# Attention with pooled upsampling and a mixer of eight batches: the scale of u from a bound in place of its largest value, and a new order table

## The chip, the cores and the metric

One core of a Trainium2 chip runs the program. The metric is the device time of one execution in microseconds; lower is better. The kernel before takes 911.1 us, the median of three runs (910.91 to 912.58).

## What is computed

For each of 8 batches the reference adds two attentions of 8 heads over 576 positions (head size 64), and runs a mixer with two pairs of matrices over the result:

```
q_d, k_d, v_d = means over groups of 4 positions (576 -> 144)
out_up    = repeat(softmax(q_d k_d^T / 8) v_d, 4)
out_local = softmax(mask(|i - j| < 4, q k^T / 8)) v
x = (out_up + out_local), laid out as 576 x 512
u = x + (relu(x^T w_tok1) w_tok2)^T          # w_tok1 576 x 256, w_tok2 256 x 576
y = u + relu(u w_ch1) w_ch2                  # w_ch1 512 x 1536, w_ch2 1536 x 512
```

All inputs and outputs are f32 in value; the weights arrive as 64-bit words and are converted on the chip.

## The kernel before

Every large product is made of three 16-bit passes (`mm3`, line 132): each operand is split into a high f16 part and a low f16 part (the rest), after it was multiplied with a power of two that keeps it in f16's range. So each operand needs a scale, and a scale needs a number that no value exceeds.

**Start.** Batch 0's attention runs while the weights load. Each weight tile is converted by `to_f32` (line 232): an activation on ScalarE, two passes on GpSimd (lines 242 and 245), one on VectorE (line 250). `token_weight` and `column_sums` make the token weights W: TensorE sums magnitudes (`W_sum`, line 304), VectorE turns the largest into a scale (`wscale`), and both split the tiles (lines 279 and 281). `load_v` squares V on ScalarE (line 503) and pools it on GpSimd (lines 507 and 508); `value_scale` (line 318) makes from it the factors `up` and `down` of a batch, and the products `av` with V (line 657) wait for them through `st.up`. `C1` and `C2` (w_ch1 and w_ch2, 12 tiles each) are converted, scaled (`root`, line 147) and split (`parts`, line 368).

**Mixer.** `mix(st)` (line 682) is the token mixing of a batch: `splits` splits x, `products` forms t1 = w_tok1 with x (line 710), `takes` writes `hid` = relu of it as two f16 parts (lines 739 and 741), `products` forms t2 on top of the transposed x (lines 723 and 728), and `takes` reads it out of PSUM as u (line 752). Batch 0 then goes on in `scaled`, the others in `mixtures`, `upper` and `lower`, which also form sums of blocks of u: batches 1 to 7 do the first channel product with seven products in place of eight (`product7`, tensors P, Q and R). `second` forms the second channel product (tensor c with weights CX), `second_up` adds u (line 1042) and stores.

**The scale of u** is the part that the change touches. Per column block c and chunk of positions ch VectorE reads all of u again for its largest magnitude:

```
nc.vector.tensor_reduce(st.umx[:, ch, c:c + 1], st.u[c][:, s0:s0 + N], axis=AX.X, op=ALU.max, apply_absolute_value=True)
```

That is 8 instructions a batch, 64 in all (line 754). `scale_of` (line 758) then makes one number of them in `everywhere` (line 666): a maximum on VectorE, a transposition on TensorE (`um_t`), a maximum of the row, a product with ones that spreads it (`um_b`), and `pow2` (line 136), three small VectorE instructions. Batch 0 does this once per chunk, the others once.

**What sets the order.** The kernel writes its instructions as some 300 streams (attention pieces b, mixer pieces n, channel pieces e, the start's A, C, D, W and others). `drive` (line 180) merges them before the program is built: it keeps a clock per engine from estimated step lengths, and of the streams that could go next at about the same time takes the one that stands first in ORDER. Each engine then executes its instructions strictly in that written order, so ORDER decides what stands behind what in each queue. Until batch 0's first scale is made, `keep_busy` puts products with `junk` (tensor `busy`, line 178) where the estimate sees TensorE idle.

Of the kernel before, what the change touches and what calls it, by code (L numbers as in the profile page):

```python
# [6 lines left out]
F32 = mybir.dt.float32  # L7
# [26 lines left out]
SWITCH = 0.1  # L34
SHARED = 1.4
ORDER = ("C1 e3.1 e5.5 e5.3 A7 e3.5 e3.3 s1 e5.0 e5.6 e5.4 D11 L1 n6.3 n7.0 b3.9 e2.4 e7.1 e3.0 e3.6 e3.4 "
# [9 lines left out]
         "b3.3 e2.2 C11 b6.5 Q0 D9 h2 C7 b5.3 N2 C2 e4.7 e3.7 e6.7 C3 e1.7 n6.5 e5.7 ").split()  # L46
# [7 lines left out]
def tile_ups_attention_mixer(ctx, tc, qk, vw, vr, w1, w2, c1, c2, out):  # L54
# [15 lines left out]
    BUFS = dict(cw=6, h=6, vm=2, bs=2, bs2=4, w=4, xh=2, x=5, u=6, uh=7, tm=6, ts=2, qk=4, qd=1, vw=2, vd=1, pt=2, od=1, sm=10, ev=4, nm=4, qs=1, sc=20)  # L70
# [89 lines left out]
    def step(engine, us, *needs, at=None, take="", give=""):  # L160
        return dict(F="P", W="V").get(engine, engine), us, needs, at, take.split(), give.split(), engine
# [156 lines left out]
    def value_scale(st):  # L318
# [6 lines left out]
        e = yield step("V", 0.8, give="g")  # L325
        root(big, 2.0 ** 20, st.big[:, 0:1], st.big[:, 1:2])
        nc.vector.tensor_mul(st.up, whole[:, 0:1], st.big[:, 1:2])
        nc.vector.tensor_mul(st.down, whole[:, 1:2], st.big[:, 0:1])
        make(("scale", b), e)
# [48 lines left out]
    class First(Channel):  # L378
# [8 lines left out]
        def scale(self):  # L387
            for q in range(NQ):
# [4 lines left out]
                root(big, 2.0 ** (4.5 + 0.5 - 8), self.inv[q], self.s[q])  # L393
# [272 lines left out]
    def everywhere(name, cols, n=128):  # L666
# [512 lines left out]
```

## Time and profile before

| what | value |
|---|---|
| median of three runs | 911.1 us |
| the profiled execution's own time | 909.63 us |
| its span, first to last instruction | 907.8 us |
| TensorE busy | 869.8 us, 96% of the span |
| VectorE busy | 551.3 us, 61% |
| ScalarE busy | 438.3 us, 48% |
| GpSimd busy | 303.2 us, 33% |
| mean granted TensorE clock | 0.985 |

A share over the whole span mixes stages with different limits, so the tables of stretches and the timelines tell more than this one. A busy TensorE is not a TensorE at its peak, and its fillers with `junk` count as busy too.

### The profile page before, as it was taken

How to read it: one execution, taken by the hardware profiler on the slowest of the kernel's cores; microseconds unless marked ns; L12 is line 12 of the kernel's file. 1: busy time of each engine (PE TensorE's matmuls, PEld its weight loads, DVE VectorE, ACT ScalarE, POOL GpSimd, SP SyncE). 2: the span in 40 equal slices, each digit the busy share in tenths (PEclk: the TensorE clock that was granted, in tenths of full speed). 3: DMA queues.
4: the chain of work that ended last, by engine and by line, in shares of the span. 5: the costliest groups of instructions: out<-in, count | busy, mean ns of one | idle time of the engine just before them, and what ended most of it. 6: DMA issues, size and time to landing. Idle time of an engine off the chain costs nothing.

```text
span 907.8 us, 26395 instructions
## 1 busy us (share of the span) xinstructions
PE 869.8 (96%) x11183; PEld 656.0 (72%) x11189; DVE 551.3 (61%) x1306; ACT 438.3 (48%) x1028; POOL 303.2 (33%) x465
## 2 busy tenths in 40 slices
PE   6877799999999999999999999999999999999998
PEld 3644568867676877777877777778877786787776
DVE  6778999678863764447653485445854584524521
ACT  4656467344663545534563455535463555503510
POOL 4779874399004420054015220054004420002000
PEclk9769999999999999999999999999999999999999
DMA  9844541363125111450156002441126211110201
GB/s 256 217 168 165 187 114 35 116 187 103 56 97 177 48 37 57 140 148 22 52 174 141 23 21 74 142 132 43 50 67 198 69 35 43 53 44 24 74 20 34
DMA packets 36870, 87.23 MB, mean 96 GB/s; under 512 B 4464, under 2 KB 17264, under 8 KB 35504
## 3 DMA queue, kind: packets, MB, share of 16 engines
q1 hardware_dynamic: 36112, 84.95, 30.7%
q8 instruction: 88, 1.44, 0.7%
q10 hardware_dynamic: 640, 0.59, 0.2%
q14 instruction: 30, 0.25, 0.1%
HBM read 71.37 MB, written 11.80 MB: 92 GB/s over the span
## 4 chain that ended last, share of the span: by engine, by line
PE 81%; DVE 11%; ACT 4%; issue 2%; DMA 1%; POOL 0%; SPq 0%; ACTq 0%; DVEq 0%; POOLq 0%
PE c L134 31%; PE P L134 13%; PE t L134 10%; PE R L134 7%; PE Q L134 3%; PE av L657 3%; PE ad L587 3%; PE t L723 2%; PE pT L644 2%; PE sc L621 2%; PE sd L559 2%; PE td L578 1%; DMA vr<-in_vr_dram 1%; DVE CX L250 1%; ACT pd L571 1%
## 5 line engine op out<-in xcount | busy, mean ns | idle before, releaser
L134 PE MATMUL c<-h,CX 128*128 128x320 f16 (+1 forms) x2304 | 296.8, 286 | 0.0
L134 PEld LDWEIGHTS <-CX 128*128 128x128 f16 x2304 | 221.4, 98 | 59.1 <-issue 4.0
L134 PEld LDWEIGHTS <-CW 128*128 128x128 f16 x1296 | 123.4, 98 | 38.9 <-issue 2.9
L533 POOL TENSOR_TENSOR qs<-qk 128x288 f32<-128x288 f32 x56 | 40.3, 719 | 246.2 <-DMA qk<-in_qk_dram 242.4
L1042 DVE SCALAR_TENSOR_TENSOR u<-c,io,u 128x256 f32<-128x256 f32 (+1 forms) x64 | 32.9, 514 | 93.0 <-PE c L134 92.3
L134 PEld LDWEIGHTS <-t 128*128 128x128 f16 x756 | 73.9, 98 | 19.3 <-issue 0.6
L507 POOL TENSOR_TENSOR vr<-vr 72x256 f32<-72x256 f32 x64 | 48.2, 754 | 77.5 <-ACT dump L503 77.0
L752 ACT ACTIVATE u<-t,down 128x256 f32<-128x256 f32 (+1 forms) x64 | 29.9, 497 | 84.2 <-PE t L134 84.2
L134 PE MATMUL t<-xh,W 128*128 128x512 f16 (+1 forms) x240 | 58.0, 379 | 0.0
L754 DVE TENSOR_REDUCE umx<-u 128x1 f32<-128x256 f32 (+1 forms) x64 | 28.0, 448 | 45.6 <-ACT u L752 45.5
L947 DVE TENSOR_TENSOR x<-x,Q 128x288 f32<-128x288 f32 x42 | 19.0, 452 | 59.7 <-PE Q L134 59.6
L134 PE MATMUL t<-W,hid 128*128 128x256 f16 (+1 forms) x384 | 53.5, 286 | 0.3 <-DVE hid L741 0.3
L571 ACT ACTIVATE pd<-sd,nmd 72x144 f32<-72x144 f32 x128 | 37.7, 373 | 33.0 <-DVE nmd L566 28.7
L503 ACT ACTIVATE dump<-vr 72x512 uint8<-72x512 f32 x64 | 40.1, 627 | 26.9 <-DMA vr<-in_vr_dram 26.4
L801 POOL TENSOR_TENSOR s<-u,u 128x288 f32<-128x288 f32 x14 | 11.1, 810 | 123.1 <-ACT u L752 123.1
L701 DVE SCALAR_TENSOR_TENSOR xh<-x,back,xh 128x512 f16<-128x512 f32 (+1 forms) x40 | 32.7, 824 | 22.5 <-ACT xh L699 22.4
L134 PEld LDWEIGHTS <-hid 128*128 128x128 f16 x384 | 36.2, 98 | 9.6 <-DVE hid L741 0.6
L587 PE MATMUL ad<-vd,ptd 72*72 72x65 f32 x512 | 40.7, 234 | 0.3 <-ACT ptd L581 0.3
L587 PEld LDWEIGHTS ad<-vd,ptd 72*72 72x72 f32 x512 | 39.0, 151 | 2.2 <-ACT ptd L581 0.8
L662 ACT ACTIVATE x<-av,up 128x512 f32<-128x512 f32 (+1 forms) x40 | 27.3, 685 | 25.1 <-PE av L657 24.7
L134 PE MATMUL P<-a22h,CW 128*128 128x288 f16 x252 | 38.0, 286 | 1.4 <-DVE m L947 1.2
L134 PEld LDWEIGHTS <-W 128*128 128x128 f16 (+1 forms) x240 | 21.9, 97 | 24.0 <-issue 3.1
(182 smaller groups left out, 1658.1 us busy)
## 6 DMA issues: line engine op xcount, KB each, us to landing
qk<-in_qk_dram SPq DMA_DIRECT2D x32, 579.0 KB
t<-sums SPq DMA_DIRECT2D x42, 384.0 KB
vw<-in_vw_dram SPq DMA_DIRECT2D x32, 351.0 KB
vr<-in_vr_dram SPq DMA_DIRECT2D x64, 144.0 KB
C_raw<-in_c_dram SPq DMA_DIRECT2D x16, 512.0 KB
out_dram<-u SPq DMA_DIRECT2D x32, 160.0 KB
C_raws<-in_c_dram SPq DMA_DIRECT2D x8, 512.0 KB
out_dram<-u SPq DMA_DIRECT2D x32, 128.0 KB
```

Source lines behind the costliest of these rows:

```text
L134: nc.tensor.matmul(ps, lhs(a), rhs(c), start=first and i == 0, stop=last and i == 2, **kw)
L503: nc.scalar.activation(dump, t.rearrange("p r c -> p (r c)"), AF.Square, scale=2.0 ** -20, accum_out=st.vm[:, i:i + 1])
L507: nc.gpsimd.tensor_add(t[:, 0:2], t[:, 0:2], t[:, 2:4])
L533: nc.gpsimd.tensor_add(two, x[:, :, 0:2], x[:, :, 2:4])
L571: nc.scalar.activation(pd[:, par, g], s[:, par, g], AF.Exp, bias=nm[:, par, g:g + 1], scale=0.125 / 16)
L587: nc.tensor.matmul(ps[:, g, par], pt[:, par, kg, G * g:G * g + G], st.vd[:, kg, 2 * pr + par], start=kg == 0, stop=kg == 1)
L657: nc.tensor.matmul(ps[QB * j:QB * j + QB, par, D * hp:D * hp + D], pt[p, hp, QB * j:QB * j + QB], st.vw[h][p, g, D * hp:D * hp + D], start ...
L662: nc.scalar.activation(x.rearrange("p hp two d -> p two hp d"), ps[:n, :, :4 * D].rearrange("p two (hp d) -> p two hp d", hp=4), AF.Copy, ...
L701: nc.vector.scalar_tensor_tensor(st.xh[t][:, 1], xf(t), back[:n], st.xh[t][:, 0], ALU.mult, ALU.subtract)
L752: nc.scalar.activation(st.u[c][:, s0:s0 + N], banks[ch, c // 2][:, c % 2, :N], AF.Copy, scale=st.down)
L754: nc.vector.tensor_reduce(st.umx[:, ch, c:c + 1], st.u[c][:, s0:s0 + N], axis=AX.X, op=ALU.max, apply_absolute_value=True)
L1042: nc.vector.scalar_tensor_tensor(u, banks[c, ch], io[:, ch:ch + 1], u, ALU.mult, ALU.add)
```

## The change

u is not read again for its largest value. u is `down` times (x and the token mixing), so a bound on it comes from numbers that are there earlier: the largest v (`big`), and the largest value of `hid` times the largest column sum of w_tok2, which `whole` already carries. `value_scale` writes two factors into a new tile `most`, and `scale_of` takes one maximum over both halves of `hid`'s high parts, spreads it as before, and forms bound = largest hid x most[1] + most[0]. One scale serves both chunks of batch 0 now. The powers of two beside it move (2^-5 to 2^-7 for u, 2^-8 to 2^-6 for C1) and so do two buffer counts. The table ORDER and the constant SWITCH, the planner's price for a change of kind on TensorE, are other ones, so nearly every engine's order changes.

```
-SWITCH = 0.1
+SWITCH = 0.05
-ORDER = ("C1 e3.1 e5.5 e5.3 A7 e3.5 e3.3 s1 e5.0 e5.6 e5.4 D11 L1 n6.3 n7.0 b3.9 e2.4 e7.1 e3.0 e3.6 e3.4 "
...
+ORDER = ("n3.2 e1.1 e3.1 e6.1 D7 b3.2 e5.1 e7.1 A2 e6.2 D4 e6.5 b6.8 b5.3 e4.1 b4.8 b6.3 n6.2 e1.4 T0 e5.2 "
...
-    BUFS = dict(... bs2=4 ... sc=20)
+    BUFS = dict(... bs2=6 ... sc=16)
...
+        st.most = T([128, 2], F32, "bs2", f"most{b}")
+        nc.vector.tensor_scalar(st.most[:, 0:1], st.big[:, 0:1], 4.0, None, ALU.mult)
+        nc.vector.tensor_scalar(st.most[:, 1:2], st.down, 516.0, None, ALU.mult)
...
-                root(big, 2.0 ** (4.5 + 0.5 - 8), self.inv[q], self.s[q])
+                root(big, 2.0 ** (4.5 + 0.5 - 6), self.inv[q], self.s[q])
...
+            st.tops = both[:, :, 0]
             make(("hid", b), e)
-            st.umx = T([128, 2, 4], F32, "sc", f"umx{b}")
...
-                    e = yield step("V", 0.05 + N * 0.00112)
-                    nc.vector.tensor_reduce(st.umx[:, ch, c:c + 1], st.u[c][:, s0:s0 + N], axis=AX.X, op=ALU.max,
-                                            apply_absolute_value=True)
...
+        def scale_of():
+            yield step("V", 0.0, ("hid", b))
+            big = yield from everywhere(f"um{b}", st.tops, 128, 1.1)
+            inv = st.ui[0] = st.ui[1] = T([128, 1], F32, "sc", f"ui{b}")
+            s = T([128, 1], F32, "sc", f"us{b}")
+            most = T([128, 1], F32, "sc", f"mu{b}")
+            yield step("V", 0.55, give="g")
+            nc.vector.tensor_scalar(most, big, st.most[:, 1:2], st.most[:, 0:1], ALU.mult, ALU.add)
+            pow2(most, 2.0 ** -7, inv, s)
+            return s
```

Three places show what the new order moves. The line numbers of the kernel after are 3 or 4 higher.

The first is GpSimd's queue at the start, from its first work on loaded data; `vr` is V (the pooling sums), `W..._raw` are the token weights (their conversion). Before:

```order
L507 TENSOR_TENSOR vr0_0_195<-vr0_0_195 72x256
L508 TENSOR_TENSOR vd0_191<-vr0_0_195 72x2x64
L242 TENSOR_SCALAR W0_raw_197<-W0_raw_197 128x256
L507 TENSOR_TENSOR vr0_1_199<-vr0_1_199 72x256
L508 TENSOR_TENSOR vd0_191<-vr0_1_199 72x2x64
L507 TENSOR_TENSOR vr0_2_206<-vr0_2_206 72x256
L508 TENSOR_TENSOR vd0_191<-vr0_2_206 72x2x64
L507 TENSOR_TENSOR vr0_3_210<-vr0_3_210 72x256
L508 TENSOR_TENSOR vd0_191<-vr0_3_210 72x2x64
```

After:

```order
L242 TENSOR_SCALAR W0_raw_195<-W0_raw_195 128x256
L245 TENSOR_SCALAR W0_raw_195<-W0_raw_195 128x256
L242 TENSOR_SCALAR W0_raw_195<-W0_raw_195 128x256
L510 TENSOR_TENSOR vr0_0_197<-vr0_0_197 72x256
L511 TENSOR_TENSOR vd0_191<-vr0_0_197 72x2x64
L245 TENSOR_SCALAR W0_raw_195<-W0_raw_195 128x256
L242 TENSOR_SCALAR W2_raw_206<-W2_raw_206 128x256 x2
L242 TENSOR_SCALAR W4_raw_232<-W4_raw_232 64x256
L245 TENSOR_SCALAR W2_raw_206<-W2_raw_206 128x256
L245 TENSOR_SCALAR W4_raw_232<-W4_raw_232 64x256
```

Of V only one tile's sums are left among the conversions, and the last conversion of a weight tile stands behind five tiles of V; before, the sums of four tiles of V (vr0 to vr3) stood ahead of the second weight tile, and the last conversion stood behind all eight.

The second is VectorE's queue in batch 0 around the scale of u; `hid0` and `u0` are batch 0's, `CW` and `CX` are the tiles of C1 and C2, `C1_inv` and `C1_s` the scale of C1's first four tiles. Before, from the first reduction of `u0` on:

```order
L754 TENSOR_REDUCE umx0_1180<-u0_0_1219 128x1
L250 SCALAR_TENSOR_TENSOR CX0_1211<-C2_raw0_1054 128x512
L250 SCALAR_TENSOR_TENSOR CX1_1212<-C2_raw1_1066 128x512
L754 TENSOR_REDUCE umx0_1180<-u0_1_1235 128x1
L374 SCALAR_TENSOR_TENSOR CW3_148<-CW4_149,C1_s0_135,CW3_148 128x512
L754 TENSOR_REDUCE umx0_1180<-u0_2_1259 128x1
L366 TENSOR_REDUCE C1_mx_131<-C1_sum4_1134 128x1
L670 TENSOR_REDUCE C1_n1_m_1275<-C1_mx_131 128x1
L754 TENSOR_REDUCE umx0_1180<-u0_3_1276 128x1
L250 SCALAR_TENSOR_TENSOR CX2_1213<-C2_raw3_1092 128x512
L676 TENSOR_REDUCE C1_n1_m1_1284<-C1_n1_t_1282 1x1
L670 TENSOR_REDUCE um0_0_m_1293<-umx0_1180 128x1
```

After, from the first of VectorE's two writes of `hid0` on:

```order
L744 SCALAR_TENSOR_TENSOR hid0_1158<-t1_0_1033,hid0_1158 128x512
L250 SCALAR_TENSOR_TENSOR CW10_155<-C19_raw_1047 128x512
L744 SCALAR_TENSOR_TENSOR hid0_1158<-t1_0_1033,hid0_1158 128x512
L149 TENSOR_SCALAR C1_inv0_132<-C1_n0_b_1167 128x1
L151 TENSOR_SCALAR C1_inv0_132<-C1_inv0_132 128x1
L152 RECIPROCAL C1_s0_135<-C1_inv0_132 128x1
L673 TENSOR_REDUCE um0_m_1198<-hid0_1158 128x1
L377 SCALAR_TENSOR_TENSOR CW0_145<-CW1_146,C1_s0_135,CW0_145 128x512
L679 TENSOR_REDUCE um0_m1_1212<-um0_t_1210 1x1
L766 TENSOR_SCALAR mu0_1228<-um0_b_1224,most0_840 128x1
L138 TENSOR_SCALAR ui0_1226<-mu0_1228 128x1
L139 TENSOR_SCALAR ui0_1226<-ui0_1226 128x1
```

The maximum over `hid0` stands right behind hid's last write, and its chain has one split of C1 (`CW0`) in it; before, the chain began behind four reductions of u with conversions of C2 between them.

The third is VectorE's queue in batch 2, after its token mixing; `u1` is batch 1's u, to which the second channel product is added. Before (the maximum `um2_0_m` that begins the chain follows 57 rows further down):

```order
L741 SCALAR_TENSOR_TENSOR hid2_4376<-t1_2_4204,hid2_4376 128x512
L1040 TENSOR_TENSOR io1_1764<-ui1_0_3499,ic_158 128x1
L1042 SCALAR_TENSOR_TENSOR u1_0_3241<-c2_1_0_0_4315,io1_1764,u1_0_3241 128x256
L741 SCALAR_TENSOR_TENSOR hid2_4376<-t1_2_4204,hid2_4376 128x512
L565 TENSOR_REDUCE mxd3_0_4410<-sd3_0_4405 72x4
L566 TENSOR_SCALAR nmd3_0_4411<-mxd3_0_4410 72x4
L754 TENSOR_REDUCE umx2_4404<-u2_0_4438 128x1
L754 TENSOR_REDUCE umx2_4404<-u2_1_4458 128x1
```

After:

```order
L744 SCALAR_TENSOR_TENSOR hid2_4338<-t1_2_4222,hid2_4338 128x512 x2
L1043 TENSOR_TENSOR io1_1828<-ui1_3076,ic_158 128x1
L1045 SCALAR_TENSOR_TENSOR u1_0_3028<-c2_1_0_0_4307,io1_1828,u1_0_3028 128x256
L673 TENSOR_REDUCE um2_m_4386<-hid2_4338 128x1
L568 TENSOR_REDUCE mxd3_0_4393<-sd3_0_4388 72x4
L569 TENSOR_SCALAR nmd3_0_4394<-mxd3_0_4393 72x4
L679 TENSOR_REDUCE um2_m1_4404<-um2_t_4402 1x1
L766 TENSOR_SCALAR mu2_4434<-um2_b_4430,most2_3695 128x1
```

The maximum of hid stands behind one addition to batch 1's u, and the whole chain to the scale now follows at once.

## Rows read from the trace of the kernel before

**Rows 1.** The page: busy tenths of TensorE in 40 slices of the span.
```profile
PE   6877799999999999999999999999999999999998
```

**Rows 2.** Stretches: us; PE, PEld, DVE, ACT, POOL busy (count); granted clock; DMA.
```profile
0.00:57.85 57.85, 42.33 (x506) 24.91 (x510) 43.94 (x106) 33.71 (x79) 39.61 (x67) 0.82 0.74 206
57.85:132.58 74.73, 61.71 (x890) 41.55 (x893) 66.72 (x134) 45.10 (x94) 60.61 (x67) 0.95 0.47 167
132.58:228.10 95.52, 94.52 (x1335) 73.04 (x1334) 77.32 (x178) 45.60 (x108) 60.99 (x97) 1.00 0.38 112
228.10:873.00 644.90, 639.82 (x8207) 492.06 (x8205) 359.15 (x883) 313.84 (x749) 141.96 (x235) 1.00 0.26 79
```

**Rows 3.** Timeline, 42 to 62 us: start, us, engine line op; idle before it.
```profile
42.26 1.28 ACTq L603 DMA_DIRECT2D vw<-od  x1
...
45.46 0.76 POOL L245 TENSOR_SCALAR W_raw<-W_raw 128x256 bf16<-128x256 f32 x1
...
50.09 1.39 PE L304 MATMUL W_sum<-W_raw,junk 128*128 128x256 bf16 x5 [2.69 <-ACT W_raw L276]
...
53.65 4.27 DVE L281 SCALAR_TENSOR_TENSOR W<-W_raw,wscale,W 128x256 f16<-128x256 f32 x5
...
57.85 0.14 DVE L670 TENSOR_REDUCE vm_m<-vm 72x1 f32<-72x8 f32 x1
...
62.05 2.05 PE L657 MATMUL av<-vw,pt 47*32 47x64 f32 x128
```

**Rows 4.** VectorE's groups by shape: count, busy us, mean ns, idle before.
```profile
L754 DVE TENSOR_REDUCE umx<-u 128x1 f32<-128x320 f32 x32 | 14.9, 482 | 27.1 <-ACT u L752 27.1
...
L754 DVE TENSOR_REDUCE umx<-u 128x1 f32<-128x256 f32 x32 | 13.1, 415 | 18.5 <-ACT u L752 18.3
...
L250 DVE SCALAR_TENSOR_TENSOR CW<-C_raw 128x512 uint32<-128x512 uint32 x12 | 10.5, 887 | 0.0
...
L281 DVE SCALAR_TENSOR_TENSOR W<-W_raw,wscale,W 128x288 f16<-128x288 f32 x4 | 3.5, 922 | 0.4 <-ACT W L279 0.4
...
L676 DVE TENSOR_REDUCE um_m<-um_t 1x1 f32<-1x128 f32 x9 | 2.5, 273 | 0.4 <-PE um_t L673 0.4
```

**Rows 5.** VectorE's groups by shape, 57.85 to 132.58 us alone.
```profile
L633 DVE TENSOR_TENSOR P<-P,mx 128x304 f32<-128x304 f32 x2 | 1.2, 620 | 0.1
...
L628 DVE TENSOR_TENSOR P<-sc,mask 128x304 f32<-128x304 f32 x2 | 0.9, 458 | 0.0
```

**Rows 6.** Timelines: TensorE around the first product with c1, VectorE at C2's scale.
```profile
96.71 1.89 PE L178 MATMUL busy<-junk 128*128 128x512 bf16 x7 [1.83 <-DVE C_inv L149]
...
99.30 1.47 PE L134 MATMUL c<-uh,CW 128*128 128x256 f16 x12
...
132.58 0.14 DVE L149 TENSOR_SCALAR ic<-C_n_b 128x1 uint32<-128x1 uint32 x1
```

**Rows 7.** Line 250 in the second stretch; lines 250 and 754: ns minimum/median/maximum.
```profile
57.85:132.58 74.73, 20.67 (x22) 0.95 0.47 167
...
L250 DVE SCALAR_TENSOR_TENSOR CW<-C_raw x12: 670/692/1559, 44.2 to 81.6; 128x512 uint32<-128x512 uint32 x12
...
L754 DVE TENSOR_REDUCE umx<-u x64: 402/443/489, 84.1 to 821.5; 128x1 f32<-128x256 f32 x32, 128x1 f32<-128x320 f32 x32
```

**Rows 8.** TensorE's timeline, 112 to 117 us.
```profile
112.82 1.80 PE L134 MATMUL c<-uh,CW 128*128 128x320 f16 x12
114.56 0.71 PE L559 MATMUL sd<-qd 64*72 64x144 f32 x8
115.20 1.80 PE L134 MATMUL c<-uh,CW 128*128 128x320 f16 x12
116.84 0.67 PE L578 MATMUL td<-ident,pd 72*72 72x72 f32 x8
```

**Rows 9.** Batch 0: last product of the token mixing, and VectorE's last write of hid.
```profile
75.52 1.62 PE L134 MATMUL t<-xh,W 64*128 64x512 f16 x6
...
79.50 0.69 DVE L741 SCALAR_TENSOR_TENSOR hid<-t,hid 128x512 f16<-128x512 f32 x1 [0.66 <-ACT hid L739]
```

More of the change, by code (lines that the diff above doesn't have):

```diff
@@ L33 @@
 HOP = 0.2
-SWITCH = 0.1
+SWITCH = 0.05
 SHARED = 1.4
-ORDER = ("C1 e3.1 e5.5 e5.3 A7 e3.5 e3.3 s1 e5.0 e5.6 e5.4 D11 L1 n6.3 n7.0 b3.9 e2.4 e7.1 e3.0 e3.6 e3.4 "
[9 rows of a table removed]
-         "b3.3 e2.2 C11 b6.5 Q0 D9 h2 C7 b5.3 N2 C2 e4.7 e3.7 e6.7 C3 e1.7 n6.5 e5.7 ").split()
+ORDER = ("n3.2 e1.1 e3.1 e6.1 D7 b3.2 e5.1 e7.1 A2 e6.2 D4 e6.5 b6.8 b5.3 e4.1 b4.8 b6.3 n6.2 e1.4 T0 e5.2 "
[9 rows of a table added]
+         "b5.0 C5 e2.7 e5.3 s0 C2 P1 e7.7 Q0 b5.5 e5.7 n2.1 e6.7 e1.7 e4.7 b2.4 ").split()
 PX = 7
@@ L69, in tile_ups_attention_mixer @@
     psum = ctx.enter_context(tc.tile_pool(name="psum", bufs=1, space=bass.MemoryType.PSUM))
-    BUFS = dict(cw=6, h=6, vm=2, bs=2, bs2=4, w=4, xh=2, x=5, u=6, uh=7, tm=6, ts=2, qk=4, qd=1, vw=2, vd=1, pt=2, od=1, sm=10, ev=4, nm=4, qs=1, sc=20)
+    BUFS = dict(cw=6, h=6, vm=2, bs=2, bs2=6, w=4, xh=2, x=5, u=6, uh=7, tm=6, ts=2, qk=4, qd=1, vw=2, vd=1, pt=2, od=1, sm=10, ev=4, nm=4, qs=1, sc=16)
     SLOTS = dict(gg=2, m=3, g=1, w=4)
@@ L324, in value_scale @@
         st.up, st.down = (T([128, 1], F32, "bs2", f"{x}{b}") for x in ("up", "down"))
-        e = yield step("V", 0.8, give="g")
+        e = yield step("V", 1.0, give="g")
         root(big, 2.0 ** 20, st.big[:, 0:1], st.big[:, 1:2])
@@ L664, in local, with everywhere @@
         make(("x", b, t), e)
-    def everywhere(name, cols, n=128):
+    def everywhere(name, cols, n=128, us=0.08, *needs):
         m = T([n, 1], F32, "ev", f"{name}_m")
-        yield step("V", 0.08)
-        nc.vector.tensor_reduce(m, cols, axis=AX.X, op=ALU.max)
+        yield step("V", us, *needs)
+        nc.vector.tensor_reduce(m, cols, axis=AX.X if len(cols.shape) == 2 else AX.XY, op=ALU.max)
         yield step("F", 0.11, take="g")
@@ L748, in takes @@
                 for c in (2 * two, 2 * two + 1):
-                    yield step("A", 0.06 + N * 0.00113, ("t2", b, ch, c), give=f"gg>{b}" if c % 2 else "")
+                    e = yield step("A", 0.06 + N * 0.00113, ("t2", b, ch, c), give=f"gg>{b}" if c % 2 else "")
                     if ch == 0:
@@ L752, in takes @@
                     nc.scalar.activation(st.u[c][:, s0:s0 + N], banks[ch, c // 2][:, c % 2, :N], AF.Copy, scale=st.down)
-                    e = yield step("V", 0.05 + N * 0.00112)
-                    nc.vector.tensor_reduce(st.umx[:, ch, c:c + 1], st.u[c][:, s0:s0 + N], axis=AX.X, op=ALU.max,
-                                            apply_absolute_value=True)
                     make(("u", b, ch, c), e)
-        def scale_of(ch, cols):
-            big = yield from everywhere(f"um{b}_{ch}", cols)
-            inv = st.ui[ch] = T([128, 1], F32, "sc", f"ui{b}_{ch}")
-            s = T([128, 1], F32, "sc", f"us{b}_{ch}")
-            yield step("V", 0.45, give="g")
-            pow2(big, 2.0 ** -5, inv, s)
+        def scale_of():
[7 more added lines that the diff above has]
+            pow2(most, 2.0 ** -7, inv, s)
             return s
@@ L768, in scaled @@
                 s0, N = CHUNKS[ch]
-                yield step("V", 0.0, *(("u", b, ch, c) for c in range(4)))
-                s = yield from scale_of(ch, st.umx[:, ch])
+                if ch == 0:
+                    s = yield from scale_of()
                 uh = st.uh[ch] = []
                 for c in range(4):
-                    yield step("A", 0.06 + N * 0.00113, *([("h", b - 1, ch, NF - 1)] if b else []))
+                    yield step("A", 0.06 + N * 0.00113, ("u", b, ch, c), *([("h", b - 1, ch, NF - 1)] if b else []))
                     if ch == 1 or c % 2 == 0:
@@ L806, in upper @@
         def upper():
+            st.us = yield from scale_of()
             yield step("V", 0.0, *all_u)
-            st.us = yield from scale_of(0, st.umx.rearrange("p a c -> p (a c)"))
-            st.ui[1] = st.ui[0]
             for name in ORDER7:
```

18 rows, old and new, of the table ORDER are left out of this document.

## Prediction

> **What bounds the kernel now.** I read the page's slices first, then a table of four stretches, then the timeline of the start, and the groups of VectorE last. The slices show TensorE at nine tenths or more from about 110 us to the end, and at six to eight tenths ahead of that [rows 1]. The stretches say the same in numbers: from 228.10 to 873 us TensorE is busy 639.82 of 644.90 us at a granted clock of 1.00, while VectorE is busy 359.15; from 132.58 to 228.10 it is busy 94.52 of 95.52. In the two stretches ahead it is not the bound: 42.33 of 57.85 us and 61.71 of 74.73, part of that fillers, and VectorE (43.94 and 66.72) and GpSimd (39.61 and 60.61) carry as much or more [rows 2]. So the kernel is a start of 132.58 us, paced by conversions on VectorE and GpSimd, and then TensorE's own work. Whatever VectorE saves behind 132.58 us is worth nothing unless TensorE waits for it; there only TensorE's work counts.
>
> I cut the start at two instructions that exist in both kernels. The first is the maximum of batch 0's V at 57.85 us: the products with V wait for what follows from it and begin at 62.05 [rows 3]. The second is the start of C2's scale at 132.58 us, the edge of the stretches, from where TensorE is full. The profiled execution took 909.63 us; its median of three is 911.1, so 1.5 is added at the end.
>
> **The change, part by part.** *Removed in the steady part.* 64 reductions of u go, 32 of 0.482 and 32 of 0.415 us, 28.0 us of VectorE in all, and one of nine chains to a scale [rows 4]. *Added:* eight maxima over hid's high parts, 128x1024 in 16 bits each, and three small instructions a batch of some 0.15 us. No reduction over 16-bit values is in this trace. Through the two reductions of u runs a line of 0.067 us more for 64 elements, 1.05 ns an element, which puts 1024 elements at 1.22 us; if 16-bit values were read faster it might be no more than two of the 256-wide reductions, 0.8. I take 1.22, since the nearest rows are of the same instruction. The Trainium skill ("VectorE: DVE Perf Modes", section on the perf-mode tier table) lists this reduction with the slowest mode alone, for every type; by that the 0.8 would drop out, and no row here shows it. Behind 132.58 us about 24 us of 28 fall away, next to a TensorE that waits 5.1 us in 645 [rows 2]: worth 0 there, bounds 0 to -2.
>
> *First piece, to V's maximum.* GpSimd's queue converts the token weights ahead of most of V's sums now, where before V stood ahead. In the timeline GpSimd's last conversion of W begins at 45.46 us, TensorE sums W at 50.09 after 2.69 us of waiting, VectorE then splits five tiles of W from 53.65 on for 4.27 us, and only behind them comes V's maximum [rows 3]. Ahead of that maximum VectorE's queue holds three instructions fewer in the new order: two conversions of C1 at 0.887 and one split of W2 at 0.922 us [rows 4], 2.7 us. Times the stretch over its busy time (57.85 / 43.94 = 1.32) that is -3.6 us. Following the chain by hand along the new queues, with the durations of the rows, V's maximum lands near 51.3 us, 6.5 earlier. Against it: the four transfers `vw`, issued from 42.26 us on and long landed before [rows 3], now stand just ahead of the products with V, whose result needs them. I take -4.5, bounds 0 and -6.5.
>
> *Second piece, to C2's scale.* VectorE's work between the two cuts, each instruction at its group's mean: eight reductions of u out, 4 x 0.482 + 4 x 0.415 = -3.6; one chain of 0.27 and three small ones out, -0.7; one maximum over hid for two small ones, 1.22 - 0.30 = +0.9; three small additions, +0.45; from the first piece two conversions of C1 and one split of W2, +2.7 [rows 4]; one split of C1 less and some writes of h more, -0.3; and two softmax tiles of batch 1, six instructions each, the first group 0.9 and the largest 1.2 us for the two, 5.4 in all [rows 5], which stand behind the cut now, where TensorE is full. The sum is -5.9, on 70.3 us by group means that took 74.73: x 1.06 = -6.3 us. The place where it is felt is the first product with c1. Before, TensorE waited 1.83 us, ran seven fillers at 96.71 us, and began that product at 99.30; C2's scale followed at 132.58 [rows 6]. In the new order those products stand directly behind the token mixing, without fillers. What speaks for less is that VectorE's time here is not all work: line 250 took 20.67 us for 22 conversions where its fastest, 0.670, would make 14.7, and it reaches 1.559 us, while reductions of u stay between 0.402 and 0.489 [rows 7]. The 6 us above the fastest are waits beside GpSimd that do not shrink with VectorE's list. I take -5.0, bounds 0 and -6.3.
>
> The Trainium skill ("SBUF — State Buffer", section "Who interferes with whom") says that a VectorE instruction with two inputs in SBUF and GpSimd's reads exclude each other, while a reduction never contends. The trace agrees, by the spread of line 250 against that of line 754 [rows 7]. It speaks against the change: what is removed are the instructions that were not in GpSimd's way.
>
> *What TensorE has left at C2's scale.* By the two queues, four more groups of c at 128x256 are done by then (1.47 each [rows 6]), two fewer at 128x320 (1.80) and five fewer f32 groups of about 0.67 [rows 8]: 3.6 + 3.4 - 5.9 = +1.1 us later. *Changes of kind.* From batch 1's first product on, TensorE's queue goes from f16 products to f32 ones 141 times, before 125. What one costs is seen only by difference: the same group of c runs 1.74 us until a product `sd` begins (112.82 to 114.56) and 1.64 until `td` does (115.20 to 116.84) [rows 8]. I take 0.10 each, +1.6; bounds 0 and +4, if a change cost the whole overlap of a group with its neighbours, about 0.23. The count of products themselves is the same.
>
> *The chain that moves earlier in TensorE's queue.* The transposition in the scale's chain now stands soon behind the token mixing. In batch 0, hid is whole 3.05 us after the mixing's last product ends (75.52 + 1.62 to 79.50 + 0.69 [rows 9]); with the maximum, 1.22, and some 0.2 between engines, 4.5 us. In five of the seven later batches 36 products of c and one `sd`, about 3 x 1.64 + 0.7 = 5.6 us at most and 5.1 at least [rows 8], stand between. That hides it, with 0.6 to 1.1 us to spare; costed at nothing.
>
> **Sum.** -4.5 - 5.0 + 1.1 + 1.6 = -6.8 us on 909.63, so 902.8; with the 1.5 to the median, **904.3 us**. This case's own range is 899 to 909.
>
> **Rivals.** *One: GpSimd paces the second piece.* If VectorE's waits beside GpSimd grow into the room that is freed, the second piece stays as long as it was. For it: GpSimd is busy 60.61 of 74.73 us there [rows 2] with the same work. Against it: TensorE's wait of 1.83 us and its fillers ended on VectorE. -4.5 + 1.1 + 1.6 = -1.8 gives 909.3. This rival is what the Trainium skill's section cited above ("SBUF — State Buffer", "Who interferes with whom") would make of the piece. Chance 0.14.
>
> *Two, slower: both start pieces keep their length.* In the first GpSimd's 39.61 us and the loads that it waits for (DMA share 0.74 [rows 2]) then set the pace, and the new order only swaps which of V and W is late; the `vw` transfers are late in place of the weights. What remains is the added work of TensorE, +1.1 + 1.6 = +2.7: 913.8. It decides once the two pieces together shorten by less than 2.7 us. Chance 0.14.
>
> *Three: TensorE waits for the scale's chain.* If the maximum over hid runs late, because an addition to the previous batch's u or a softmax stands ahead of it, or it takes 1.9 and not 1.22 us, the cover is used up and TensorE stands about 0.7 us in each of seven batches: +4.9, so 909.2. Against it: VectorE is busy 56% of that stretch [rows 2]. Chance 0.12.
>
> **How the numbers follow.** The forecast has 0.60. A measurement of this kernel can tell about 0.2%, 1.8 us, from no change, so faster begins below 909.3 and slower above 912.9. Faster: 0.57 of the forecast's 0.60 and half of rivals one and three, 0.13, together 0.70. Slower: most of rival two, 0.13. The rest, 0.17, is no change. The range of 898.5 to 912 takes in the forecast's bounds, rivals one and three, and leaves out rival two and the forecast's far tails.
>
> **What would show it.** Right: in the new profile the products with V begin near 58 us (62.05 before), c1's first product follows the token mixing without fillers, C2's scale is made near 123 us (132.58), and from there to the end the time is some 2.7 us longer than before with TensorE waiting about 5 us in the steady part. Wrong: C2's scale at 130 us or later, GpSimd's conversions as the releaser of VectorE's waits, or waits of TensorE ahead of the transpositions `um_t` of several us in sum. A maximum over hid at 0.8 us would leave the sum as it is; one near 2 us would bring rival three.

## The result and the profile after

The kernel after takes 900.97 us, the median of four executions (900.7 to 902.88), beside 911.0 for the kernel before, measured with it: a ratio of 0.9892 (95% interval 0.9873 to 0.991). The forecast was 904.3, faster, with a range from 898.5 to 912. Run again later it took 902.85 (seven executions) beside 909.81, a ratio of 0.9936 (0.9914 to 0.9959), so the gain is 7 to 10 us.

Single executions of either kernel differ by some us, mostly in the start: before took 903.1 to 913.7 us over 21 executions on one chip, and in six profiles of kernels that are the same from C2's scale on that part takes 773.2 to 774.5 us, while V's maximum moves by 3 us (table below). The profile of after is of the slowest of its four (902.88 us, span 901.0), that of before of one 1.4 us under its median. So the two profiles differ by 6.8 us where the medians differ by 10.0. The sum of the prediction was made against the profiled execution, and that is what its steps are compared with; the other runs show how far each stretch varies.

The page, after: TensorE's busy time, its slices and its granted clock, beside [rows 1].

```profile
PE 868.9 (96%) x11178; PEld 655.9 (73%) x11185; DVE 550.8 (61%) x1261; ACT 437.7 (49%) x1028; POOL 310.6 (34%) x465
...
PE   6888799999999999999999999999999999999998
...
PEclk9789999999999999999999999999999999999999
```

VectorE's busy time is nearly the same as before (551.3 us), although 28 us of reductions went: the new maxima took 9.7 of it back, and 12.1 went into three groups of splits in batches 1 to 7 (`a11h`, `s1h`, `a12h`), which run longer at the same count. The first of them, before and after:

```profile
L826 DVE SCALAR_TENSOR_TENSOR a11h<-u,us,a11h 128x288 f16<-128x288 f32 x14 | 6.7, 510 | 2.6 <-ACT a11h L817 2.6
L829 DVE SCALAR_TENSOR_TENSOR a11h<-u,us,a11h 128x288 f16<-128x288 f32 x14 | 12.3, 914 | 19.9 <-ACT a11h L820 19.9
```

Before, no GpSimd instruction ran beside any of the fourteen. After, the scale is there earlier, and all but one of them run beside GpSimd's sums of blocks of u (line 805). TensorE is full there, and this costs nothing that the time shows.

The same cuts as in [rows 2], at V's maximum, at C2's scale and near the end (columns: stretch, us, then busy time of PE, PEld, DVE, ACT, POOL with counts, granted clock, DMA):

```profile
0.00:53.44 53.44, 41.06 (x500) 23.59 (x507) 40.39 (x103) 32.17 (x76) 31.14 (x60) 0.84 0.70 198
53.44:126.50 73.06, 61.02 (x711) 42.04 (x711) 63.48 (x117) 39.54 (x79) 61.24 (x63) 0.93 0.50 177
126.50:222.00 95.50, 94.45 (x1426) 72.20 (x1424) 79.98 (x176) 51.88 (x121) 66.21 (x100) 1.00 0.41 116
222.00:866.20 644.20, 640.95 (x8296) 493.57 (x8295) 362.75 (x861) 314.08 (x756) 152.02 (x245) 1.00 0.26 80
```

The first piece is 4.4 us shorter, the second 1.7, and from C2's scale to the end it is 774.5 us, where it was 907.8 - 132.58 = 775.2: another 0.7. The first piece's timeline, GpSimd's last pass over a weight tile ahead of the first sums, TensorE's last sum of W, VectorE's splits, V's maximum and the first product with V, to be read against [rows 3]:

```profile
41.30 0.83 POOL L245 TENSOR_SCALAR W_raw<-W_raw 128x288 bf16<-128x288 f32 x1
...
46.17 1.19 PE L304 MATMUL W_sum<-W_raw,junk 128*128 128x288 bf16 x4
...
52.58 0.93 DVE L281 SCALAR_TENSOR_TENSOR W<-W_raw,wscale,W 128x288 f16<-128x288 f32 x2
53.44 0.15 DVE L673 TENSOR_REDUCE vm_m<-vm 72x1 f32<-72x8 f32 x1
...
59.12 1.48 PE L660 MATMUL av<-vw,pt 47*32 47x64 f32 x128
```

The last pass over W begins 4.2 us earlier, the last sum 3.9, V's maximum 4.4 and the products with V 2.9. In the second piece c1's first product stands behind the token mixing without fillers, as the order said, at 90.31 in place of 99.30 [rows 6], and TensorE then waits:

```profile
88.67 1.80 PE L134 MATMUL t<-W,hid 128*128 128x320 f16 x12
90.31 2.90 PE L134 MATMUL c<-uh,CW 128*128 128x256 f16 x24
93.04 0.39 PE L388 MATMUL C_sum<-CW 128*128 128x128 bf16 x4
93.48 0.38 PE L178 MATMUL busy<-junk 128*128 128x512 bf16 x1
96.66 0.60 PE L134 MATMUL c<-uh,CW 128*128 128x256 f16 x4 [2.80 <-DVE h L880]
```

Of the 9 us by which that product is earlier, C2's scale is 6.1 earlier (126.50). The maximum over hid took what the line through the two reductions said, 1.21 us for 1.22 (nanoseconds minimum, median, maximum):

```profile
L673 DVE TENSOR_REDUCE um_m<-hid x8: 1200/1207/1210, 77.9 to 787.5; 128x1 f32<-128x1024 f16 x8
```

### The profile page after: what moved, and what is told of

It reads as the page before. It is cut to its first block, busy times and chain, and to the rows that moved or that the text cites. A ratio compares the mean times of both kernels' runs of the same rounds, so it can differ in the third digit from the quotient of the medians.

```text
span 901.0 us, 26344 instructions
## 1 busy us (share of the span) xinstructions
PE 868.9 (96%) x11178; PEld 655.9 (73%) x11185; DVE 550.8 (61%) x1261; ACT 437.7 (49%) x1028; POOL 310.6 (34%) x465
## 4 chain that ended last, share of the span: by engine, by line
PE 82%; DVE 10%; ACT 3%; issue 2%; DMA 2%; POOL 1%; DVEq 0%; ACTq 0%; POOLq 0%
PE c L134 31%; PE P L134 13%; PE t L134 10%; PE R L134 6%; PE Q L134 3%; PE ad L590 3%; PE av L660 3%; PE sc L624 2%; PE t L726 2%; PE sd L562 2%; PE td L581 2%; PE pT L647 2%; PE busy L178 1%; DMA vw<-od 1%; DVE CW L377 1%
## 5 line engine op out<-in xcount | busy, mean ns | idle before, releaser
L755 ACT ACTIVATE u<-t,down 128x256 f32<-128x256 f32 (+1 forms) x64 | 29.8, 497 | 96.4 <-PE t L134 96.2
L134 PE MATMUL c<-uh,CW 128*128 128x256 f16 (+1 forms) x288 | 40.3, 294 | 7.0 <-DVE h L880 5.6
L631 DVE TENSOR_TENSOR P<-sc,mask 128x304 f32<-128x304 f32 (+1 forms) x40 | 18.7, 467 | 38.7 <-PE sc L624 38.7
L134 PE MATMUL Q<-a12h,CW 128*128 128x288 f16 x252 | 38.0, 286 | 1.3 <-DVE u L1045 1.0
```

What stands on the lines that cost most here:

```text
L134: nc.tensor.matmul(ps, lhs(a), rhs(c), start=first and i == 0, stop=last and i == 2, **kw)
L755: nc.scalar.activation(st.u[c][:, s0:s0 + N], banks[ch, c // 2][:, c % 2, :N], AF.Copy, scale=st.down)
```

## The experiments

Since executions vary, the runs are compared by stretches first: V's maximum, the second piece from there to C2's scale, and the rest to the end of the span, each from one profile. Totals are medians of the executions.

```
kernel                     V's maximum  2nd piece   rest    total   ratio to before (95%)
before                        57.85       74.7     775.2
before, again                 59.4        75.6     775.5
after                         53.44       73.1     774.5   900.97  0.9892 (0.9873-0.9910)
after, again                  51.2        73.3     773.7   902.85  0.9936 (0.9914-0.9959)
8 reductions, batch 0         50.9        76.3     773.3   906.09  0.9980 (0.9955-1.0005)
8 splits twice, batch 0       50.6        77.9     773.2   906.71  0.9983 (0.9958-1.0009)
12 GpSimd passes out          53.1        71.0     774.2   899.23  0.9889 (0.9846-0.9932)
56 reductions, splits         53.5        73.9     782.3   908.67  1.0005 (0.9980-1.0031)
56 reductions, earlier        51.0        73.8     775.3   901.95  0.9931 (0.9910-0.9952)
maximum twice, batches 1-7    50.9        72.5     774.1   903.78  0.9950 (0.9923-0.9976)
ten fillers                   52.5        75.0     774.5   901.80  0.9916 (0.9891-0.9942)
new scale, old table          56.2        96.5     765.6   919.77  1.0126 (1.0094-1.0158)
old scale, new table          54.1        86.1     810.3   950.08  1.0443 (1.0407-1.0479)
V ahead of W on GpSimd        60.0        74.4     785.0   921.46  1.0142 (1.0094-1.0189)
```

The ratios are to executions of before that were taken with the run. Down to the ten fillers all from "after" on have the order of after, with instructions added or left out; the last three are planned anew, and their C2's scale stands elsewhere in the work, so that for them only the first column can be compared. Between V's maximum and C2's scale six of the profiles hold the same work (the two of after, both with 56 reductions, the doubled maximum and, but for the fillers, the ten fillers): there the second piece takes 72.5 to 75.0 us, 73.6 in the mean. A difference of 2 us in one profile is hardly clear of that.

**The two kernels again.** After:

> The kernel after, unchanged, for more executions of it beside the other runs and a second profile. The start of one execution varies by some us (in the runs so far the order up to V's maximum is the same and it comes at 50.9 to 53.5 us), so totals need many executions. Expected by what was measured first: 7 to 10 us faster than the kernel before; C2's scale at 123 to 127 us, 72 to 74 us behind V's maximum; from there to the end 774 to 775 us.

Before:

> The kernel before, unchanged, for a second profile of its start. Expected from the profile that the prediction was made from, and from what the kernel after shows of an execution's own variation: V's maximum at 56 to 59 us, C2's scale 74 to 75.5 us behind it, and 774.5 to 776 us from there to the end.

Nearly all of it came out within these bounds: V's maximum and the second piece of before (59.4, 75.6) and the rest of after (773.7) lie a few tenths outside. The nine kernels with the order of after have V's maximum at 50.6 to 53.5 us, 51.9 in the mean, the two profiles of before at 57.85 and 59.4. So the first piece's gain is 6.7 us by these means, rather than the 4.4 of the one pair; two profiles of before are few, and single pairs lie between 4.3 and 8.8.

**Does VectorE's list pace the second piece?** Eight reductions of u put back in batch 0:

```diff
                     nc.vector.scalar_tensor_tensor(o[:, 1], u, s, o[:, 0], ALU.mult, ALU.subtract)
+                    nc.vector.tensor_reduce(spare[:, 4 * ch + c:4 * ch + c + 1], u, axis=AX.X, op=ALU.max,
+                                            apply_absolute_value=True)
```

> The kernel after, in its own order, with the eight removed reductions of u put back in batch 0 alone, each right behind the split of the same piece of u, so that none waits for anything new; nothing uses their results. They are worth 4 x 0.482 + 4 x 0.415 = 3.6 us of VectorE in the second start piece. Theory (VectorE's list paces that piece, as the prediction has it): 2.5 to 4 us slower than the kernel after. Rival (GpSimd and its loads pace it): 0 to 0.7 us.

The second piece took 76.3 us, 3.0 to 3.2 more than the two profiles of after and 1.3 more than the slowest of the six. The total is 2.3 us above that of the doubled maximum on the same chip (906.09 and 903.78). So of 3.5 us of list (the rows) 2 to 3 us cost time, as the theory says: VectorE's list paces most of the piece.

```profile
L786 DVE TENSOR_REDUCE spare<-u 128x1 f32<-128x320 f32 x4 | 1.9, 473 | 0.0
L786 DVE TENSOR_REDUCE spare<-u 128x1 f32<-128x256 f32 x4 | 1.6, 406 | 0.0
```

**Two inputs in place of one.** A version with a maximum of u with itself, two inputs in place of the reduction's one, needed more room in SBUF than there is, so it has no time. In its place, the split itself twice:

```diff
                     nc.vector.scalar_tensor_tensor(o[:, 1], u, s, o[:, 0], ALU.mult, ALU.subtract)
+                    nc.vector.scalar_tensor_tensor(o[:, 1], u, s, o[:, 0], ALU.mult, ALU.subtract)
```

> The kernel after, in its own order, with each of the eight splits of u in batch 0 written twice (the same instruction again, two inputs in SBUF; alone it takes 0.47 and 0.58 us, the reductions of the earlier run 0.41 and 0.47). Theory (such instructions wait for GpSimd there, reductions do not): the second start piece, 72.4 to 74 us in the kernels with the order of after and 76.3 with the eight reductions, takes 78.5 to 82 us, with the doubled splits near 1 us each. Rival (VectorE's time alone counts): 76.5 to 77.5 us, as 4.2 us of work beside the 3.6 of the reductions.

77.9 us: between the two expectations. VectorE's groups by shape in that run, sixteen splits:

```profile
L784 DVE SCALAR_TENSOR_TENSOR uh<-u,us,uh 128x256 f16<-128x256 f32 x4 | 3.4, 859 | 0.0
L784 DVE SCALAR_TENSOR_TENSOR uh<-u,us,uh 128x320 f16<-128x320 f32 x4 | 3.4, 851 | 0.0
L785 DVE SCALAR_TENSOR_TENSOR uh<-u,us,uh 128x320 f16<-128x320 f32 x4 | 2.9, 721 | 0.1
L785 DVE SCALAR_TENSOR_TENSOR uh<-u,us,uh 128x256 f16<-128x256 f32 x4 | 2.9, 718 | 0.1
```

They took 12.6 us, where the eight of after took 8.2: 4.4 us for eight more. The piece is 4.6 to 4.8 us longer than in the two profiles of after, and the total 4.9 us above that of the ten fillers on the same chip. They are not near 1 us each, but in the mean all four groups stand well above the fastest such splits in the timeline of after (0.47 us for 128x256, 0.58 for 128x320), while the reductions stood at 0.41 and 0.47. So an instruction with two inputs does cost more beside GpSimd, though less than I had put on it.

**GpSimd relieved.** The first pass over C2's tiles left out:

```diff
-        nc.gpsimd.tensor_scalar(lo, lo, 2.0 ** -29, -0.501, ALU.mult, ALU.add)
+        if not c2:
+            nc.gpsimd.tensor_scalar(lo, lo, 2.0 ** -29, -0.501, ALU.mult, ALU.add)
```

> The kernel after, in its own order, without GpSimd's first pass over the twelve tiles of C2 (the shift of the lower words is left out, so C2 is wrong): 12 x 0.7 = 8.4 us of GpSimd's 61 us in the second start piece. Theory (VectorE's list paces that piece, and GpSimd only makes VectorE's two-input instructions wait): 71 to 73 us in place of 73.3, by shorter splits and conversions. Rival (GpSimd's queue paces the piece): 70 us or less.

71.0 us, at the edge of the theory's interval and 1.5 below the fastest of the six. GpSimd's busy time fell by 7.2 us (61.24 to 54.08), not by the 8.4 expected, and the piece is 2.1 to 2.4 us shorter than in the two profiles of after. In this stretch (columns as above) and in the splits:

```profile
53.10:124.10 71.00, 59.99 (x711) 41.47 (x710) 57.71 (x117) 39.28 (x79) 54.08 (x51) 0.95 0.51 182
```
```profile
L785 DVE SCALAR_TENSOR_TENSOR uh<-u,us,uh 128x320 f16<-128x320 f32 x4 | 3.4, 857 | 0.0
L785 DVE SCALAR_TENSOR_TENSOR uh<-u,us,uh 128x256 f16<-128x256 f32 x4 | 2.7, 684 | 0.0
```

VectorE's busy time fell by 5.8 us, from 63.48 to 57.71, with the same 117 instructions, and the eight splits from 8.2 to 6.1; the six profiles have 61.2 to 65.2 and 7.3 to 8.2. So part of VectorE's time there is waiting for GpSimd that counts as busy. The piece gained less than half of the 5.8: VectorE's idle time grew, among it 3.7 us of waits for GpSimd's conversions, which the ten fillers' profile has too and the first of after has not. So GpSimd's queue can pace a part of the piece, as the rival had it for the whole. And of the gain 0.8 us can be TensorE's clock, which stayed at 1.00 in this profile and not in those of after (see the fillers below).

**The steady part.** 56 reductions of u put back in batches 1 to 7, between the splits that feed the first products of a batch:

```diff
                     nc.vector.scalar_tensor_tensor(o[:, 1], blocks()[name][i], st.us, o[:, 0], ALU.mult, ALU.subtract)
+                    j = 2 * ORDER7.index(name) + i
+                    if j < 8:
+                        s0, N = CHUNKS[j // 4]
+                        nc.vector.tensor_reduce(spare[:, j:j + 1], st.u[j % 4][:, s0:s0 + N], axis=AX.X, op=ALU.max,
+                                                apply_absolute_value=True)
```

> The kernel after, in its own order, with the 56 removed reductions of u put back in batches 1 to 7, each behind a VectorE instruction that already reads u; nothing uses their results. 25 us of VectorE. Theory (TensorE is full there and hides it): within 1 us of the kernel after. Rival (VectorE is near enough to the bound that its reductions cost something, and the change's gain came from there): 3 us slower or more.

And the same 56 where the kernel before had them, behind ScalarE's reading of u:

```diff
                     nc.scalar.activation(st.u[c][:, s0:s0 + N], banks[ch, c // 2][:, c % 2, :N], AF.Copy, scale=st.down)
+                    if b:
+                        if old is not None:
+                            nc.vector.tensor_reduce(spare[:, 0:1], old, axis=AX.X, op=ALU.max, apply_absolute_value=True)
+                        old = st.u[c][:, s0:s0 + N]
```

> The kernel after, in its own order, with the 56 reductions of u put back in batches 1 to 7 not between the splits of u, as in the earlier run that lost about 8 us behind C2's scale, but where the kernel before had them, behind ScalarE's reading of u and ahead of the splits. Theory (what cost the earlier run was the delay of the splits that TensorE's next products wait for; where the reductions stood before, they were hidden): from C2's scale to the end 774 to 776.5 us. Rival (TensorE is not covered any more in the new order, wherever they stand): 779 us or more.

The first missed its theory: 782.3 us behind C2's scale, 8 more. The second kept it: 775.3 us, and a total that cannot be told from after's on the same chip (901.95 and 902.85). So the 25 us of VectorE were hidden where they stood, but for 1 to 2 us at most (773.2 to 774.5 us without them), and the steady part gained little or nothing from their going; between the splits the same work is on TensorE's path. What TensorE waited for in the first of the two, from 222 us on (total, times, longest), and the granted clock around the longest wait (stretch, us, TensorE's busy time, clock, DMA):

```profile
PE Q L134 <- DVE u L1051: 2.6, 1, 2.6
PE td L582 <- ACT pd L575: 2.0, 1, 2.0
PE c L134 <- DVE u L1051: 1.7, 2, 1.1
```
```profile
220.00:224.00 4.00, 1.74 (x15) 1.00 0.00 0
224.00:232.00 8.00, 7.64 (x101) 0.57 0.34 102
232.00:240.00 8.00, 8.00 (x100) 1.00 0.14 40
```

TensorE stood still for 2.6 us once, in batch 1, and in the 8 us behind it ran at 0.57 of its clock, most of them at the lower of its two levels, 1.2 GHz: 8 x 0.43 = 3.4 us more. TensorE's busy time behind C2's scale agrees, 770.0 us for 766.8 in after with the same products. That one wait is 6 of the 8 us in this profile. The wait of 2.0 us, at 743 us, left the clock at 1.00. In the kernel after, whose waits in this part are 1.0 us at most, the clock is 1.00 from 222 to 866 us. The profile is of an execution 2.9 us above its median; by medians on the same chip the run is 4.9 us above the doubled maximum.

**The chain to the scale.** The maximum over hid twice in batches 1 to 7:

```diff
+        if len(cols.shape) == 3 and name != "um0":
+            nc.vector.tensor_reduce(spare[:, 0:1], cols, axis=AX.XY, op=ALU.max)
         nc.vector.tensor_reduce(m, cols, axis=AX.X if len(cols.shape) == 2 else AX.XY, op=ALU.max)
```

> The kernel after, in its own order, with the maximum over hid made twice in batches 1 to 7 (1.2 us more in the chain to each scale; the first result is not used). Theory (TensorE's other products cover the chain by 0.6 to 1.1 us, as the prediction has it): TensorE waits 0.1 to 0.6 us in each batch ahead of the transposition um_t, and the kernel is 0.7 to 4 us slower. Rival (the cover is much larger): within 0.5 us.

774.1 us behind C2's scale, as in after. From there on TensorE waited ahead of the transposition once, for 0.5 us:

```profile
PE um_t L679 <- DVE um_m L676: 0.5, 1, 0.5
```

The cover is 1.2 us or more in six of seven batches: the rival was right, and what stands between in TensorE's queue hides more than I had counted.

**One half of the change alone.** The new scale with the old table, and then the old scale with the new table (the other way round, in the kernel before, with its buffer counts):

```diff
-SWITCH = 0.05
+SWITCH = 0.1
-ORDER = ("n3.2 e1.1 e3.1 e6.1 D7 b3.2 e5.1 e7.1 A2 e6.2 D4 e6.5 b6.8 b5.3 e4.1 b4.8 b6.3 n6.2 e1.4 T0 e5.2 "
...
+ORDER = ("C1 e3.1 e5.5 e5.3 A7 e3.5 e3.3 s1 e5.0 e5.6 e5.4 D11 L1 n6.3 n7.0 b3.9 e2.4 e7.1 e3.0 e3.6 e3.4 "
...
```

> The new scale of u with the old table, the old price SWITCH and the new buffer counts; the planner lays the streams out anew, since the steps differ, so this order was searched for neither kernel. Theory (the second start piece is paced by VectorE's list, and what the scale takes off it is worth 3 us there; the first piece is the order's): V's maximum comes at 55 us or later, the second piece takes 70 to 73 us, and the rest from C2's scale on is as long as before (775 us) or longer by what the unsearched order leaves. Rival (the new order alone makes the gain): the second piece takes 75 us or more, and the whole is no faster than before.

> The old scale of u with the new table and the new SWITCH, in the old buffers; the planner lays the streams out anew here too. Theory: the first piece is the order's, so V's maximum comes at 51 to 54 us as in the kernel after; the second piece takes 75 us or more, since the reductions of u are in it, and the whole lies between the two kernels or above before. Rival (the new scale makes all of the gain): V's maximum at 57 us or later, and no gain at all.

Neither gains: 1.3% and 4.4% slower than before. Each table was searched for one stream of steps, and with other steps the planner makes an order that nobody has searched. The second pieces (96.5 and 86.1 us) end at another place of the work and decide nothing on the theory about them, though by the letter the first run met its rival (75 us or more, no faster). The first column does say something: with the old table and the new scale V's maximum comes at 56.2, with the new table and the old scale at 54.1, just above the expected 51 to 54. GpSimd's queue at the start is that of before in the one and that of after in the other, so most of this gain goes with the table.

**W and V on GpSimd.** The plan holds the weight tiles back until V is pooled:

```diff
-        yield step("G", 0.34 + n * 0.00127)
+        yield step("G", 0.34 + n * 0.00127, *hold)
...
-        yield from to_f32(raw, made["W", "raw", i])
+        yield from to_f32(raw, made["W", "raw", i], hold=[("v", 0, 2)] if i else [])
```

> The kernel after, in which the plan holds GpSimd's conversion of all weight tiles but the first until three tiles of V are pooled; in the resulting queue four tiles of V stand ahead of the second weight tile, as in the kernel before. The planner lays everything else out anew, so only the first start piece is compared. Theory (the order of weights and V on GpSimd makes the first piece's gain): V's maximum at 55 us or later, beside 50.6 to 53.5 in the kernels with the order of after, and GpSimd's last pass over a weight tile of 128x256 at 44 us or later. Rival (VectorE's own list, three instructions shorter, makes it): V's maximum still at 50.6 to 53.5.

GpSimd's last pass over W at the start (over a tile of 128x288, as in after; the last over a tile of 128x256 begins at 26.22), TensorE's last sum of W, and V's maximum:

```profile
45.93 0.97 POOL L245 TENSOR_SCALAR W_raw<-W_raw 128x288 bf16<-128x288 f32 x1
```
```profile
51.81 0.93 PE L304 MATMUL W_sum<-W_raw,junk 128*128 128x288 bf16 x3 [0.31 <-ACT W_raw L276]
```
```profile
60.01 0.14 DVE L673 TENSOR_REDUCE vm_m<-vm 72x1 f32<-72x8 f32 x1
```

V's maximum is back at 60.0 us, later than in either profile of before. Pass, sum and maximum move together, as the theory says: with V ahead of W on GpSimd the maximum comes 6.5 us or more behind that of the nine. The maximum alone does not decide against the rival, since VectorE's list ahead of it grew again in this plan, by three conversions of C1 and one split of W. The sum does. It begins at 51.81 us here and at 50.09 and 51.66 in the profiles of before, but at 42.7 to 46.8 in the nine; from the sum to the maximum, where the splits of W stand, it is 8.2, 7.8 and 7.7 us, and 6.7 to 8.2 in the nine. So nearly all of the difference arises ahead of the sum. Not separated is a third thing that the new table moved: ahead of the last pass over W GpSimd had 3.4 us of passes over C1 before, 0.7 after, and none in this run.

**Fillers in the second piece's wait.** Ten more products with junk ahead of the third product with c1:

```diff
+            if b == 0 and ch == 0 and f == 2 and free["g"]:
+                keep_busy(10)
             ps = PM(f"c1_{b}_{ch}_{f}")[:, :N]
```

> The kernel after with ten more products with junk in TensorE's queue, ahead of the third product with c1, where TensorE waited 2.8 us for VectorE's h and then ran at a granted clock of 0.70 and 0.87 for 8 us. If the lower clock costs time there: the clock stays at 1.00 from 96 to 104 us and the kernel gains 0.5 to 1.5 us over the kernel after. If VectorE's list covers it: within 0.5 us, which a total cannot tell, with C2's scale as late behind V's maximum as before, 72.4 to 74 us.

The clock, after first, then with the fillers:

```profile
92.00:96.00 4.00, 1.81 (x17) 1.00 0.01 2
96.00:100.00 4.00, 3.34 (x20) 0.70 0.08 9
100.00:104.00 4.00, 3.83 (x29) 0.87 0.67 253
```
```profile
92.00:96.00 4.00, 3.89 (x34) 1.00 0.00 0
96.00:100.00 4.00, 3.56 (x23) 1.00 0.01 2
100.00:104.00 4.00, 3.30 (x30) 1.00 0.58 190
```

The product that stood behind the wait, after first, then with the fillers:

```profile
96.66 4.40 PE L134 MATMUL c<-uh,CW 128*128 128x256 f16 x24 [2.80 <-DVE h L880]
98.60 2.78 PE L134 MATMUL c<-uh,CW 128*128 128x256 f16 x24 [0.44 <-DVE h L882]
```

The clock held, and the 24 products took 2.78 us in place of 4.40. From the start of these products C2's scale follows after 28.9 us, where it was 29.8 in both profiles of after. Two profiles without the fillers (the doubled maximum, and the 56 reductions put back earlier) have the same wait of 2.8 us, but the clock stayed at 1.00, and there it is 29.0 and 28.9. So the lower clock costs 0.8 to 0.9 us here, within the first case's 0.5 to 1.5. The total, 901.80 us, cannot tell that, and the second piece as a whole was outside what was expected, 75.0 us: from V's maximum to c1's first product, ahead of the fillers, it took 39.7 us in this execution and 36.9 to 37.9 in the other five of the six. No version that was run is faster than after by more than the intervals.

## Why the prediction was right, and where it was off

The sum of -6.8 us met the 6.8 between the two profiles, but that is luck: errors of some us cancel in it, and the profile of after is that of its slowest execution. By the means of all profiles that can be compared, the three parts are -6.7, -1.6 and -1.4 us, -9.7 in all, where the two pairs of medians have -10.0 and -7.0. Of the signs named, c1's first product does follow the token mixing without fillers, C2's scale comes at 126.50 (near 123), the products with V begin at 59.12 (near 58), and TensorE waits 3.3 us in the steady part (about 5); the 2.7 us more behind C2's scale did not come.

- **First piece, taken as -4.5: measured -4.4** in the pair of profiles, and -6.7 by the means of the nine kernels with that order and the two profiles of before. The mechanism is shown in the main: with V ahead of W on GpSimd again the last sum of W is late again, and V's maximum with it. The prediction put 3.6 us on VectorE's list ahead of the maximum; the stretch from the sum to the maximum, where most of that list would show, is only 0.5 us shorter (7.8 to 7.3). The chain followed by hand along the queues (51.3 us) was nearer to the nine (51.9) than the lower value that I chose. The products with V gained 2.9 in the pair, against 4.4 for the maximum, but the `vw` transfers that the prediction had against it are not shown as the cause: only 0.2 us of TensorE's waits are put down to them. Between the maximum and those products stand more fillers than before, and at a lower clock:

```profile
58.78 1.01 PE L178 MATMUL busy<-junk 128*128 128x512 bf16 x2 [0.37 <-DVE vm_m L676]
55.01 1.83 PE L178 MATMUL busy<-junk 128*128 128x512 bf16 x4 [0.31 <-DVE vm_m L679]
```

  The first line is of before, the second of after, where the granted clock from 54 to 57 us was 0.56.
- **Second piece, taken as -5.0: measured -1.7** in the pair, 1.4 to 2.6 by the two profiles of each. This is the term that was off. It took VectorE's list to be 5.9 us shorter at the groups' mean times and scaled that up. The list did pace most of the piece (the eight reductions, 3.5 us, cost 2 to 3), but its instructions did not keep their durations. VectorE's busy time fell by 3.2 only, from 66.72 to 63.48, and its idle time grew by 1.6. The eight splits of u, all of them two-input instructions, take 8.2 us in after:

```profile
L784 DVE SCALAR_TENSOR_TENSOR uh<-u,us,uh 128x320 f16<-128x320 f32 x4 | 4.2, 1053 | 0.0
L784 DVE SCALAR_TENSOR_TENSOR uh<-u,us,uh 128x256 f16<-128x256 f32 x4 | 4.0, 1000 | 0.0
```

  They took 6.8 before, where three ran beside GpSimd's conversions and four beside shorter GpSimd sums; now seven run beside the conversions, and the eighth, in a pause of GpSimd, took 0.47 us. The twelve conversions of C1 (line 250) took 12.1 us, 1.02 each, where the prediction had 0.887. VectorE's waits for the chain to u's scale grew from 0.8 us to 2.0 (the first and the last line), and one of 1.0 us came for the chain to a scale of C1 (the second line). From VectorE's waits between the two cuts:

```profile
DVE mu L766 <- PE um_b L682: 1.2, 1, 1.2
DVE C_n_m L679 <- PE C_n_t L676: 1.0, 1, 1.0
DVE um_m L679 <- PE um_t L676: 0.8, 1, 0.8
```

  So rival one, VectorE's waits beside GpSimd growing into the freed room, held a good part of the truth. The Trainium skill ("SBUF — State Buffer", section "Who interferes with whom") states that a reduction never contends with GpSimd on this chip, and that a VectorE instruction with two inputs in SBUF contends with a GpSimd instruction that reads SBUF; the reductions at 0.41 and 0.47 us, the doubled splits at 0.72 to 0.86 and the splits' fall from 8.2 to 6.1 with less GpSimd work agree.
- **TensorE's work left, +1.1: measured +1.0**, busy time behind C2's scale 766.8 against 765.8.
- **Changes of kind, +1.6: not seen.** The +1.0 is all that TensorE's busy time grew by, and the left-over work alone was forecast at +1.1; so the lower bound, 0, fits best. No run varied these changes by themselves. The difference of 0.10 us between two followers of the same group is no sign of their price.
- **Idle behind C2's scale, taken as unchanged: 9.5 before, 7.7 after.** With the two points above the rest came out at -0.7 where +2.7 was forecast.
- **The removed reductions in the steady part, taken as 0: shown within the spread**, 775.3 us with the 56 back in their place, 1 to 2 us more at most.
- **The chain of the scale, costed at nothing: shown**, with a larger cover than forecast.
- **Rival two** fell: both pieces shortened, by 6.1 us in the pair. **Rival three** fell with the doubled maximum.

What stays open is the split of the medians' 7 to 10 us between the order and the new scale. Only the first piece goes clearly with the table; the runs with one half of the change lose to unsearched orders and cannot divide the rest.

## What to carry to other kernels

Price a removal by the stretch in which the work stood on the path: 25 us of removed reductions were worth little or nothing under a full TensorE, and 3.5 us of the same reductions cost 2 to 3 us in the start. When an engine's list gets shorter, do not price what is left at its mean: look at which instructions share something with another busy engine, and which waits that were covered come to light. An order that was searched belongs to the code that it was searched with; changing one of the two alone lost 1 to 4% here.

## What the hardware showed beyond that

A single wait of TensorE of 2.6 us in the full part was followed by 8 us at 0.57 of the clock, which cost 3.4 us beyond the wait itself. A wait alone does not settle it: the same wait of 2.8 us in the start was followed by a granted clock below 1.00 in three profiles (the two of after, and the 56 reductions between the splits) and by 1.00 in two. The lower clock cost 0.8 to 0.9 us there. The splits `a11h` took 0.51 us in the mean where no GpSimd instruction ran beside them and 0.91 beside GpSimd's sums, while batch 0's eight reductions in the kernel before, seven of them beside GpSimd's conversions, stayed between 0.40 and 0.48 us. The maximum over 1024 16-bit values took 1.21 us, on the line of the reductions of 256 and 320 32-bit values (0.415 and 0.482 us): 16-bit inputs were read no faster. The Trainium skill ("VectorE: DVE Perf Modes", section on the perf-mode tier table) says so for this instruction, and the trace agrees.
